# Attention feeding a leaky-ReLU MoE layer on one core: blocks of two query chunks, PV for two steps at once, k turned 128 rows a transfer, batch 0 turned by TensorE

## The chip, the cores and the metric

One core of one Trainium2 chip. The metric is the device time of one execution in microseconds (us); a kernel's time is the median of its runs. A profile is of one execution and gives a span a little shorter than that execution's time (599.0 of 600.70 us in after). Five engines work side by side: TensorE (PE in profile lines, its weight loads PEld), VectorE (DVE), ScalarE (ACT), GpSimd (POOL) and SyncE (SP), which issues most transfers (280 of the 328 listed for before).

A run counts as slow when it is over 1.5% above the fastest of the same kernel. Ratios use fast runs alone; where a profile fell in a slow run, the text says so.

## The reference

```python
# q, k, v: [8 batches, 8 heads, 576, 64] f32; tau = 0.02; w_in [512, 2048], w_out [2048, 512]
scores = q @ k.transpose(0, 1, 3, 2) / sqrt(64)
thresh = scores.max(-1, keepdims=True) - tau
scores = where(scores >= thresh, scores, -1e9)
attn   = exp(scores - scores.max(-1, keepdims=True))
attn   = attn / (attn.sum(-1, keepdims=True) + 1e-09)
x      = (attn @ v)              # heads side by side: 4608 tokens x 512
h      = x @ w_in
out    = maximum(0.01 * h, h) @ w_out
```

## The kernel before

The unit of work is a **step**: one pair of heads against 128 query rows (a *chunk*). A batch has 4 pairs x 4 chunks, and 2 steps for the 64 rows that are left over: 18 steps a batch, 144 in all. In every step TensorE does the scores; VectorE takes the row maximum and masks; ScalarE does the exponentials into `W`; a DMA transpose turns `W` into `wt`; four steps later (`LAG`) TensorE multiplies `wt` by v ("PV"). The products of finished chunks are the tokens of the MoE layer. Its matmuls fill up the steps: a *hidden unit* (`hp`, 16 matmuls and a ReLU) and an *output unit* (`op`, 4 or 5 matmuls) a step.

Each f32 value of q and k is split in two f16 halves (`qs`, `ks`), three products of which make the scores, and these too are turned by DMA transposes (`qst`, `kst`). `0.99 * relu(h) + 0.01 * h` is the leaky ReLU. In most groups the second term is folded into weights: `w_io = 0.01 * w_in @ w_out` is computed once (`wiop`) and the output unit adds `x @ w_io` (`op<-wio,xT`). Early groups, before `w_io` is ready, add it on VectorE (`leak`).

```python
    LAG = 4
    NWT = 2          # blocks of wt
    def turn(nm, b, p):                     # one pair of heads, 64 rows, of q or k
        hb, g = divmod(p, 2)
        t = sb.tile([128, 2, 576], FP16, tag=nm + "st", bufs=8, name=nm + "st")
        nc.sync.dma_start(out=t.rearrange("p s (t r) -> p (s t) r", r=64),
            in_=split_tile(nm, b, hb)[ds(64 * g, 64)].rearrange("p s t h d -> p (s t h d)"), transpose=True)
    # ... cut
    def h_unit(G, u):
        def mms():
            # ... cut
            hp = ps.tile([128, 4, 128], FP32, tag="h", bufs=2, name="hp")
            for jj in range(4):
                for g in range(4):
                    mm(hp[:, jj, :], w_in16[:, g, ts(4 * u + jj, 128)], G.x[:, g, :], g == 0, g == 3)
    # ... cut
    for b in range(1, B):                   # preparation of batch b during batch b - 1
        s0 = 18 * (b - 1)
        for hb in range(2):                 # two halves: pairs 0, 1 and pairs 2, 3
            # ... cut: loads of k and q
            t0 = s0 + 1 + 8 * hb
            at(t0, lambda b=b, hb=hb: hi("k", b, hb))
            at(t0 + 2, lambda b=b, hb=hb: hi("q", b, hb))
            i = 1
            for nm in "kq":
                # ... cut: the low halves on GpSimd, i += 2 for each of two heads
                for p in (2 * hb, 2 * hb + 1):
                    at(t0 + i + p % 2, lambda nm=nm, b=b, p=p: turn(nm, b, p))
        for i in range(4):
            at(s0 + 6 + i, lambda b=b, i=i: load_v(b, i))
    # ... cut: the loop over steps; turn_w(s - 1) and pv(s - LAG) in step s
    while hq or oq:                         # the tail: MoE units that are left
        for nx in (next_o, next_h):
            # ... cut
```

Counting it out for the second half: the q transposes of pairs 2 and 3 are issued at `s0 + 18` and `s0 + 19`, which are the first and second step of the batch that uses pair 2 in its third step.

Of the kernel before, what the change touches and what calls it, by code (L numbers as in the profile page):

```python
# [16 lines left out]
def kernel(  # L17
# [19 lines left out]

    nc = tc.nc
# [6 lines left out]
    LAG = 4  # L45
    L1_GROUPS = set(range(8, 36))
    WIO = 20
    NJ = DF // 128
    NEG = -1025.0
    NW = 4  # L50
    NG = 3
# [16 lines left out]
    w_io16 = sb.tile([128, 4, DM], FP16, name="wio16")  # L68

# [43 lines left out]
    def split_tile(nm, b, hb):  # L113
        store = kss if nm == "k" else qss
        if (b, hb) not in store:
            store[b, hb] = sb.tile([128, 2, 9, 2, 64], FP16, tag=nm + "s", bufs=NSPL, name=nm + "s")
        return store[b, hb]

    def views(nm, b, hb, i, part, rows):
        m = (kms if nm == "k" else qms)[b, hb]  # L120
        s_ = split_tile(nm, b, hb)
        t0, n, odd = part
        src = m[rows, :, ds(64 * t0, 64 * n)].rearrange("p h (t d) -> p h t d", d=64)
        if odd is None:
            dst = s_[rows, i, :, :, :]
        else:
            dst = s_[rows, i, odd : 2 * n - 1 + odd : 2, :, :]
        return src, dst.rearrange("p t h d -> p h t d")

    NSPL = 2  # L130
    ALL = ds(0, 128)

    def hi(nm, b, hb, rows=ALL, eng="act"):
        for part in PARTS[nm]:
            src, dst = views(nm, b, hb, 0, part, rows)
            if eng == "act":
                nc.scalar.activation(out=dst, in_=src, func=AF.Copy, bias=0.0, scale=64.0)  # L137
            else:
                nc.vector.tensor_scalar(out=dst, in0=src, scalar1=64.0, scalar2=None, op0=AX.mult)

    def x64(nm, b, hb, h, rows=ALL):
        m = (kms if nm == "k" else qms)[b, hb][rows, h, :]
        return nc.gpsimd.tensor_scalar(out=m, in0=m, scalar1=64.0, scalar2=1.0, op0=AX.mult, op1=AX.mult)  # L143

    def lo(nm, b, hb, h, part, rows=ALL, eng="pool"):
        src, dst = views(nm, b, hb, 1, part, rows)
        _, h_ = views(nm, b, hb, 0, part, rows)
# [5 lines left out]
    def turn(nm, b, p):  # L153
        hb, g = divmod(p, 2)
        t = sb.tile([128, 2, 576], FP16, tag=nm + "st", bufs=8, name=nm + "st")
        nc.sync.dma_start(  # L156
            out=t.rearrange("p s (t r) -> p (s t) r", r=64),
            in_=split_tile(nm, b, hb)[ds(64 * g, 64)].rearrange("p s t h d -> p (s t h d)"), transpose=True)
        (ksts if nm == "k" else qsts)[b, p] = t


    class Group:


        def __init__(self, rows):
            self.l1 = len(groups) in L1_GROUPS
            self.x = sb.tile([128, 4, 128], FP16, tag="xT", bufs=5, name="xT")
            self.g = None
            self.rows = rows
# [3 lines left out]
    live_g = [0]  # L173

    def next_h():

        if hq and (hq[0][1] > 0 or live_g[0] < NG):
            f, u = hq.popleft()
            if u == 0:
                live_g[0] += 1  # L180
            return f
        return None

    def next_o():
        if oq:
            f, last = oq.popleft()
            if last:
                live_g[0] -= 1
            return f
        return None  # L190
    late = []
    leaky = []

    def leak():
        for gv, hp in leaky:
            nc.vector.scalar_tensor_tensor(out=gv, in0=hp, scalar=0.01, in1=gv, op0=AX.mult, op1=AX.add)  # L196
        leaky.clear()

    tail = [False]
    def mm(out_, lhsT, rhs, start, stop):  # L200
        nc.tensor.matmul(out=out_, lhsT=lhsT, rhs=rhs, start=start, stop=stop, skip_group_check=True)  # L201

    def h_unit(G, u):
        def mms():
            if u == 0:
                G.g = sb.tile([128, NJ, 128], FP16, tag="gT", bufs=NG, name="gT")
            hp = ps.tile([128, 4, 128], FP32, tag="h", bufs=2, name="hp")
            for jj in range(4):
                for g in range(4):
                    mm(hp[:, jj, :], w_in16[:, g, ts(4 * u + jj, 128)], G.x[:, g, :], g == 0, g == 3)  # L210

            def act():
                gv = G.g[:, ds(4 * u, 4), :]
                nc.scalar.activation(out=gv, in_=hp, func=AF.Relu, bias=0.0, scale=0.99)  # L214
                if not G.l1:
                    leaky.append((gv, hp))
                if u == 3:
                    for c in range(4):
                        oq.append((lambda c=c: o_unit(G, c), c == 3))
# [3 lines left out]
    def o_unit(G, c):  # L223
        if c == 0:
            n = len(late) % 3 if tail[0] else 2
            late.append(0)
            if n < 2:
                G.op = ps.tile([128, 2, 512], FP32, tag=f"sc{n}", bufs=1, name="op")[:, 0, :]
            else:
                G.op = ps.tile([128, 512], FP32, tag="o", bufs=1, name="op")  # L230
        if G.l1:
            mm(G.op, G.x[:, c, :], w_io16[:, c, :], c == 0, False)
        for j in range(4 * c, 4 * c + 4):
            mm(G.op, G.g[:, j, :], w_out16[:, j, :], j == 0 and not G.l1, j == NJ - 1)
        if c == 3:
            op = G.op

            def fin():
                osb = sb.tile([128, 512], FP32, tag="osb", bufs=3, name="osb")
                if tail[0]:  # L240
# [3 lines left out]
                return lambda: nc.sync.dma_start(out=G.rows, in_=osb)  # L244
            return fin
# [316 lines left out]
```

## Time and profile before

Median of the first three runs: 627.69 us (626.74 to 628.02).

From the start times of `bb`, the small VectorE instruction that negates the row maximum once a step, the trace gives the time of every stage:

| stage | us |
|---|---|
| start to first `bb` | 18.4 |
| batch 0 | 88.6 |
| batch 1 | 79.7 |
| batches 2 to 7 (to the last `bb`) | 406.9 (67.4, 70.5, 72.0, 67.2, 69.1, 60.8) |
| tail (last `bb` to the end) | 32.9 |

The page of before: span, busy time of TensorE, and, in 40 slices, the granted clock of TensorE and the busy share of the DMA engines in tenths; last, the shares of the chain of work that ended last.

```profile
span 626.5 us, 16727 instructions
...
PE 521.8 (83%) x6576; PEld 343.0 (55%) x6576; DVE 445.5 (71%) x1385; ACT 441.8 (71%) x950; POOL 144.6 (23%) x196
...
PEclk9999989898997999899997998999996999899999
DMA  7999999899999999979998999989997999866631
...
PE 46%; DMA 24%; DVE 16%; ACT 8%; SPq 4%; issue 2%; ACTq 0%; DVEq 0%
```

TensorE leads, DMA is nearly always busy, and the clock row has dips all the way: in the trace they are ten stretches from 76.5 to 544.1 us, each 3.4 to 10.2 us long with a granted clock of 0.50, and each begins during, or at most 1.4 us after, a stretch of 2.2 to 3.9 us in which TensorE stood idle.

A step without a stall, in before's timeline of TensorE (columns: start, duration, engine, line, operation, operands, shape, count):

```profile
360.37 0.47 PE L324 MATMUL pv<-wt,v 128*64 128x128 f16 x10
360.77 0.39 PE L201 MATMUL op<-wio,xT 128*128 128x512 f16 x1
361.00 1.03 PE L201 MATMUL op<-wout,gT 128*128 128x512 f16 x4
361.86 1.06 PE L201 MATMUL hp<-xT,win 128*128 128x128 f16 x16
362.85 0.91 PE L300 MATMUL sc<-kst,qst 64*128 64x288 f16 x12
```

The groups follow each other without a gap: about 3.3 us. Here is the start of a batch in the same view:

```profile
333.56 1.62 PE L300 MATMUL sc<-kst,qst 64*128 64x288 f16 x12 [3.34 <-DMA qst<-qs]
...
336.19 1.91 PE L201 MATMUL op<-wout,gT 128*128 128x512 f16 x4
```

The bracket says that TensorE stood idle for 3.34 us until a q transpose landed. After it the same four output matmuls take 1.91 us, not 1.03. The clock in the trace goes with that: from 332.5 us on, the granted clock was 0.50 for 6.8 us. "Cold" and "half clock" mean such stretches here.

Waits of before (engine, line, waited-for: us in total, times, longest), and the issues of weight transposes (count, median us from issue to landing):

```profile
PE pv L324 <- DMA wt<-w: 40.3, 21, 9.0
...
PE sc L300 <- DMA qst<-qs: 21.4, 7, 3.9
```

```profile
wt<-w SPq DMA_TRANSPOSE x144, 4.2
```

Two groups of VectorE and a stretch of the tail:

```profile
L482 DVE TENSOR_SCALAR P<-sf,mx 128x576 f16<-128x576 f32 x144 | 75.0, 521 | 0.0
...
L336 DVE TENSOR_TENSOR xT<-pv,wt 128x512 f16<-128x512 f32 x32 | 23.3, 727 | 10.7 <-PE pv L324 10.7
```

```profile
607.78 0.38 PE L201 MATMUL op<-wio,xT 128*128 128x512 f16 x1
...
608.86 1.06 PE L201 MATMUL hp<-xT,win 128*128 128x128 f16 x16
609.76 0.38 PE L201 MATMUL op<-wio,xT 128*128 128x512 f16 x1
```

A pair of hidden and output unit takes 1.98 us in the tail (607.78 to 609.76), without a wait.

### The profile page before, as it was taken

The page shows a single profiled execution, that of the slowest core. Times are in us where ns is not written, and L with a number is a line of the kernel's source. Part 1 is how long each engine was busy: PE and PEld are TensorE (multiplying, and loading weights), DVE is VectorE, ACT ScalarE, POOL GpSimd, SP SyncE. Part 2 cuts the span into 40 slices and gives each one's busy share as a digit, 9 for nine tenths or more (in the row PEclk, how much of TensorE's full clock was granted, in tenths as well). Part 3 has the DMA queues.
Part 4 walks back from the last instruction along what each step waited for, and adds up shares of the span by engine and source line. Part 5 has one row for each costly group of instructions (what it writes and reads, how often), then busy time and mean ns, then how long its engine had stood idle before and what let it go on. Part 6 is the DMA issues. An engine that isn't in the chain of part 4 may idle for free.

```text
span 626.5 us, 16727 instructions
## 1 busy us (share of the span) xinstructions
PE 521.8 (83%) x6576; PEld 343.0 (55%) x6576; DVE 445.5 (71%) x1385; ACT 441.8 (71%) x950; POOL 144.6 (23%) x196
## 2 busy tenths in 40 slices
PE   0352698889997998798897998798988999899997
PEld 0131465545564665465565665565655666566664
DVE  4462679784796998577874886687884888688810
ACT  3171578775786897688875996788876988688831
POOL 0162422131221432033311331133311432000000
PEclk9999989898997999899997998999996999899999
DMA  7999999899999999979998999989997999866631
GB/s 198 162 203 199 207 200 186 175 197 194 167 190 162 178 189 205 162 167 172 189 187 157 175 183 209 160 170 174 194 189 159 180 176 167 135 121 128 118 61 50
DMA packets 300046, 106.47 MB, mean 170 GB/s; under 512 B 274880, under 2 KB 287168, under 8 KB 299968
## 3 DMA queue, kind: packets, MB, share of 16 engines
q1 hardware_dynamic: 286912, 96.50, 85.6%
q0 software_dynamic: 13056, 8.92, 11.3%
q8 instruction: 51, 0.84, 0.6%
q14 instruction: 27, 0.22, 0.1%
HBM read 36.70 MB, written 9.44 MB: 74 GB/s over the span
## 4 chain that ended last, share of the span: by engine, by line
PE 46%; DMA 24%; DVE 16%; ACT 8%; SPq 4%; issue 2%; ACTq 0%; DVEq 0%
DMA wt<-w 17%; PE op L201 16%; PE hp L201 12%; PE sc L300 9%; DVE sf L359 8%; PE pv L324 5%; DMA qst<-qs 5%; SPq L156 3%; ACT w L473 3%; ACT P L484 2%; PE wiop L201 2%; DVE P L469 2%; DVE gT L196 2%; PE sc L306 1%; ACT qs L137 1%
## 5 line engine op out<-in xcount | busy, mean ns | idle before, releaser
L359 DVE TENSOR_SCALAR_CACHE_REDUCE sf<-sc 128x576 f32<-128x576 f32 x288 | 206.5, 755 | 114.3 <-PE sc L300 104.8
L473 ACT ACTIVATE w<-P 128x576 f16<-128x576 f16 x288 | 193.5, 675 | 24.8 <-DVE P L469 17.3
L300 PE MATMUL sc<-kst,qst 64*128 64x288 f16 x1536 | 129.6, 304 | 52.8 <-DMA kst<-ks 23.0
L201 PEld LDWEIGHTS <-win 128*128 128x128 f16 x2304 | 147.9, 101 | 35.6 <-issue 4.4
L484 ACT ACTIVATE P<-sf,bb 128x576 f16<-128x576 f32 x144 | 111.5, 774 | 71.8 <-DVE bb L480 66.7
L201 PE MATMUL hp<-xT,win 128*128 128x128 f16 x2304 | 159.7, 225 | 0.0
L201 PE MATMUL op<-wout,gT 128*128 128x512 f16 x576 | 155.1, 393 | 0.2 <-ACT osb L243 0.2
L214 ACT ACTIVATE gT<-hp 128x512 f16<-128x512 f32 x144 | 85.2, 592 | 54.6 <-PE hp L201 52.0
L300 PEld LDWEIGHTS <-qst 64*128 64x128 f16 x1536 | 70.1, 99 | 86.1 <-DMA qst<-qs 35.6
L324 PE MATMUL pv<-wt,v 128*64 128x128 f16 (+1 forms) x1600 | 72.0, 226 | 46.3 <-DMA wt<-w 40.3
L324 PEld LDWEIGHTS <-v 128*64 128x64 f16 x1600 | 51.3, 115 | 82.2 <-issue 71.9
L201 PEld LDWEIGHTS <-gT 128*128 128x128 f16 x576 | 55.3, 100 | 55.0 <-issue 7.2
L482 DVE TENSOR_SCALAR P<-sf,mx 128x576 f16<-128x576 f32 x144 | 75.0, 521 | 0.0
L469 DVE TENSOR_SCALAR P<-P 128x1152 int16<-128x1152 int16 x144 | 66.2, 460 | 9.3 <-ACT P L484 4.0
L149 POOL TENSOR_TENSOR ks<-km,ks 128x320 f16<-128x320 f32 (+1 forms) x56 | 39.8, 730 | 83.7 <-DVE P L469 55.8
L473 ACT ACTIVATION_READ_ACCUMULATOR w<-P 128x1 f32 x288 | 54.8, 190 | 0.0
L143 POOL TENSOR_SCALAR km<-km 128x576 f32<-128x576 f32 x28 | 18.7, 669 | 150.8 <-ACT ks L137 109.8
L149 POOL TENSOR_TENSOR qs<-qm,qs 128x576 f16<-128x576 f32 x28 | 35.8, 1278 | 64.7 <-DVE P L469 37.8
L201 PE MATMUL op<-wio,xT 128*128 128x512 f16 x112 | 44.8, 400 | 1.0 <-ACT osb L243 0.8
L489 DVE TENSOR_SCALAR w<-rc 128x128 f16<-128x128 f32 x144 | 32.6, 227 | 5.0
L143 POOL TENSOR_SCALAR qm<-qm 128x576 f32<-128x576 f32 x28 | 18.7, 669 | 65.4 <-DVE P L469 65.4
L336 DVE TENSOR_TENSOR xT<-pv,wt 128x512 f16<-128x512 f32 x32 | 23.3, 727 | 10.7 <-PE pv L324 10.7
(30 smaller groups left out, 254.8 us busy)
## 6 DMA issues: line engine op xcount, KB each, us to landing
km<-in_k_dram SPq DMA_DIRECT2D x16, 576.0 KB, 5.3
qm<-in_q_dram SPq DMA_DIRECT2D x16, 576.0 KB, 5.4
out_dram<-osb SPq DMA_DIRECT2D x36, 256.0 KB, 3.4
v<-in_v_dram POOLq DMA_DIRECT2D x16, 160.0 KB, 5.2
wt<-w SPq DMA_TRANSPOSE x144, 4.2
v<-in_v_dram POOLq DMA_DIRECT2D x16, 128.0 KB, 5.2
win<-in_moe_w_in_dram POOLq DMA_DIRECT2D x8, 256.0 KB, 10.1
wout<-in_moe_w_out_dram POOLq DMA_DIRECT2D x8, 256.0 KB, 10.4
```

The lines of the kernel that those rows point to most:

```text
L143: return nc.gpsimd.tensor_scalar(out=m, in0=m, scalar1=64.0, scalar2=1.0, op0=AX.mult, op1=AX.mult)
L149: return nc.gpsimd.tensor_tensor(out=dst[:, h], in0=src[:, h], in1=h_[:, h], op=AX.subtract)
L201: nc.tensor.matmul(out=out_, lhsT=lhsT, rhs=rhs, start=start, stop=stop, skip_group_check=True)
L214: nc.scalar.activation(out=gv, in_=hp, func=AF.Relu, bias=0.0, scale=0.99)
L300: nc.tensor.matmul(out=sc[h][:, half, 0:288], lhsT=qsts[b, p][r, qi, ds(128 * c, 128)], rhs=ksts[b, p][r, ki, ks_], start=(i == 0), stop=( ...
L324: nc.tensor.matmul(out=pvp[ds(64 * h, 64), p + u, :], lhsT=vt[:, p + u, h, j, :], rhs=wt[:, 4 * h + j, ds(64 * u, n)], start=(j == 0), sto ...
L359: nc.vector.tensor_scalar(out=halves(sf), in0=sc[:, :, 0:288], scalar1=C, scalar2=None, op0=AX.mult, op1=AX.max, accum_out=mx)
L469: anchor[0] = nc.vector.tensor_scalar(out=pi, in0=pi, scalar1=NEG, scalar2=None, op0=AX.max)
L473: nc.scalar.activation(out=e["W"][:, ds(576 * h, 576)], in_=e["P"][:, h, :], func=AF.Exp, bias=exp_bias, scale=1.0, accum_out=sm[:, h : h ...
L482: nc.vector.tensor_scalar(out=d["P"][:, 0, :], in0=sa, scalar1=ma, scalar2=tau_f, op0=AX.subtract, op1=AX.add)
L484: nc.scalar.activation(out=d["P"][:, 1, :], in_=sB, func=AF.Identity, bias=bb, scale=1.0)
L489: nc.vector.tensor_scalar(out=e["W"][:, 1152:1280].rearrange("p (h r) -> p h r", h=2), in0=rc.unsqueeze(2).to_broadcast([128, 2, 64]), sca ...
```

## The change

The intent: fewer and larger instructions and transposes, and q and k of the next batch turned longer before their use. From batch 2 on, two neighbouring chunks of a head pair form one unit of two steps: their `W` are turned by one transpose of 2560 columns, multiplied by v in one go (10 matmuls of 256 columns for two steps, not 20 of 128), and their tokens form one MoE group of 256 (8 matmuls of 256 columns to a hidden unit, not 16 of 128). k is turned 128 rows a transfer (two pairs at once); q stays at 64. The preparation of the next batch is laid out anew. For the second half the last two q transposes stand at `s0 + 17` and `s0 + 18`, one step earlier than before (those of the first half stand two steps later). A unit takes two steps, so pair 2 is first used in the fifth step of a batch, no longer in the third. Batch 0's q and k are turned by TensorE (`tp`). The fold of the leak stays, and its range hardly moves (from batch 2, before from the last chunk of batch 1). The 256-token hidden unit has one PSUM buffer, where hidden units had two. `xT` is evacuated per head pair and chunk (128 times), not per chunk (32 times).

```diff
-    L1_GROUPS = set(range(8, 36))
-    WIO = 20
+    L1_FROM = 2
+    WIO = 21
+    PREP = 6
+    NWT = 4
+    WOUT = 1
 ... cut
+        if nm == "k":
+            nc.sync.dma_start(
+                out=t.rearrange("p s t g r -> p (s t) (g r)"), in_=s_.rearrange("p s t h d -> p (s t h d)"),
+                transpose=True)
+        else:
+            nc.sync.dma_start(
+                out=t[:, g].rearrange("p s t r -> p (s t) r"),
+                in_=s_[ds(64 * g, 64)].rearrange("p s t h d -> p (s t h d)"), transpose=True)
 ... cut: turn_pe, eight TensorE transposes of batch 0 and their evacuations
-            hp = ps.tile([128, 4, 128], FP32, tag="h", bufs=2, name="hp")
-            for jj in range(4):
+            hp = ps.tile([128, nj, G.n], FP32, tag="hy"[u % 2] if G.n == 128 else "h", bufs=1, name="hp")
+            for jj in range(nj):
 ... cut
+        blocks = [(0, 1), (2, 3), (4,)]
+        if b < L1_FROM:
+            blocks = [(0,), (1,), (2,), (3,), (4,)]
+        elif b == B - 1:
+            blocks = [(0, 1), (4,), (2,), (3,)]
 ... cut
-            t0 = s0 + 1 + 8 * hb
+            t0 = s0 + PREP + (5 if b >= L1_FROM else 3) * hb
 ... cut: k transposes at t0 + 3, q transposes at t0 + 6 and t0 + 7
-            at(s0 + 6 + i, lambda b=b, i=i: load_v(b, i))
+            at(max(s0 + 10, 12) + i, lambda b=b, i=i: load_v(b, i))
 ... cut
+        last = units[ui][3] + size[ui] - 1
+        pv_at.setdefault(EARLY.get(ui, last + LAG), []).append(ui)
 ... cut
+            uwt[done] = sb.tile([128, 2, 10, 128], FP16, tag="wt", bufs=NWT, name="wt")
+            nc.sync.dma_start(
+                out=uwt[done][:, 0:nw].rearrange("p i j r -> p (i j) r"), in_=W_.rearrange("p i c -> p (i c)"),
+                transpose=True)
```

## The prediction

> **What bounds the kernel now.** From the timeline and the spacing of the row-maximum negations (bb, one a step, 144 steps):
> (a) Where nothing stalls, a step takes 3.3 us and TensorE is full: scores 0.83, PV 0.41, one output unit 1.09, one hidden unit 0.99. VectorE and ScalarE are busy about 2.9 us a step. 144 x 3.32 = 478 us.
> (b) Batches 2 to 7 take 67.4, 70.5, 72.0, 67.2, 69.1, 60.8 us against 18 x 3.3 = 59.4. Mostly at batch starts: the second and third steps take 7 to 9 and 4 to 5 us, because the last q transposes are issued one step before use (chain of waits at 328.8 us: DMA qst<-qs 4.75 us), and matmuls after it run cold (four output matmuls 1.91 us, not 1.03). [...] About 7 us a batch; the rest is waits for wt<-w.
> (c) Batch 0 takes 88.6 us, batch 1 79.7: first scores at 15.2 us, then steps of 7 to 11 us while q/k transposes, weight loads and wt transposes share the DMA engines (chain: wt<-w 28 us from 39 us on). Batch 1 also holds about 15 us of weight product (wiop).
>
> DMA is nearly full (slices at 9). The trace's 256-byte packets take 18 ns in the 128-row wt transposes (about 210 GB/s, 1.55 us a step) but 28 to 31 ns while only 64-row q/k transposes run (140 GB/s, 2.2 us each).
>
> **What the change does.**
> - Batch 0 turned by TensorE: eight 2.2 us transposes leave the start; v and w_in loads start at about 7 us instead of 20 to 35. Costs evacuations on ScalarE and VectorE. First scores at about 12.5 us. Gain, estimate: 20 us.
> - q/k preparation moves ahead: the last q transpose lands some 4 steps before use, so (b)'s 7 us should vanish. With new waits, batches 2 to 7 take about 62 us (the last 58). Gain 39 us, the largest term.
> - k at 128 rows: two 2.2 us transposes become one of about 2.8 us, 3 us less DMA a batch. [...]
> - PV of two steps at once, 256-token hidden matmuls: same streamed columns, half the weight loads[...]. Estimate 0.1 us a step, to 3.2; included above.
> - Leak in weights: as before in effect.
> - Tail (33 us after the last bb): 256-token groups arrive in bursts, single hidden buffer: +2 us.
> - Batch 1: less q/k contention: -4 us.
>
> Sum: 627 - 39 - 20 - 4 + 2 = 566; fewer cold stretches: 563.
>
> **Predicted: 563 us, 8 in 10 between 540 and 590. Faster 0.95, same 0.04, slower 0.01.**
>
> **What would show it.** Spacing of bb: no 7 to 9 us step at batch starts, steady steps 3.15 to 3.25, batch 0 at 60 to 70 us; qst waits near zero; TensorE busy about 88%; kst issues landing in 5 to 6 us; the chain's DMA share falling from 24% to about 12%.
>
> **What would make it wrong.** A 2560-column wt transpose (about 3.1 us) queued behind q/k transposes and loads may reach PV late, turning the removed stall into wt waits (590). The single hidden buffer may make TensorE wait for ScalarE's Relu. Or DMA is no bound and steps reach 3.1 us (540).

The sum: 627 - 39 - 20 - 4 + 2 = 566, and 563 with the 3 us for fewer cold stretches. The 2.8 and 3.1 us for larger transposes are estimates from the 18 ns packets (210 GB/s) of before's trace; the 0.1 us a step and the 3 us are estimates, which no run had measured.

## The result, and the profile after

After: 601.46 us (597.31 to 604.79, 4 runs); before beside it: 627.22 us (624.33 to 628.02, 4 runs). Ratio 0.9594, 95% interval 0.9525 to 0.9663: faster, but the time lies outside the predicted range of 540 to 590. A ratio is the mean time of one kernel's fast runs over the mean of the other's fast runs of the same rounds, so not quite the ratio of the medians quoted.

| stage | before | after | difference | predicted |
|---|---|---|---|---|
| start and batch 0 | 107.0 | 89.9 | -17.1 | -20 |
| batch 1 | 79.7 | 86.6 | +6.9 | -4 |
| batches 2 to 7 | 406.9 | 380.7 | -26.2 | -39 |
| tail | 32.9 | 41.9 | +9.0 | +2 |
| sum (span) | 626.5 | 599.0 | -27.5 | -61, and -3 for fewer cold stretches |

The stage times contain the cold stretches, so that last term has no row of its own.

The page of after, the lines shown of before:

```profile
span 599.0 us, 14446 instructions
...
PE 512.1 (85%) x5500; PEld 317.1 (53%) x5500; DVE 459.4 (77%) x1395; ACT 440.5 (74%) x948; POOL 148.7 (25%) x198
...
PEclk9999999989999999999999999999999999999999
...
PE 43%; DVE 23%; DMA 23%; ACT 7%; issue 3%; SPq 1%; ACTq 0%
```

The DMA share of the chain stays where it was (24% and 23%); the prediction expected it to halve. VectorE's share grows from 16% to 23%. (The clock row of this one run is the best of the four; the other runs of after had mean clocks of 0.947 to 0.956, against 0.991 here, and times of 597 to 605 us on both sides of it. The mean clock alone does not order the runs. In the profiles of a_noleak and a_blk1, with means of 0.958 and 0.948, the clock of batch 0 was 0.79 and 0.75, and batch 0 was no longer for it.)

Waits and transposes of after:

```profile
PE pv L386 <- DMA wt<-w: 31.9, 18, 5.4
...
PE hp L228 <- ACT gT L242: 6.9, 6, 1.8
...
PE sc L355 <- DMA qst<-qs: 4.4, 1, 4.4
```

```profile
wt<-w SPq DMA_TRANSPOSE x92, 5.1
```

As predicted, the wait of the scores for q nearly vanishes: 21.4 us in 7 waits became 4.4 in one, in batch 1. On average over batches 2 to 7, the q of pair 2 landed 11.5 us after the last `bb` of the batch before, and 6.8 us after it in the new kernel, where it is also used two steps later. But PV still waits 31.9 us for turned weights, and a wait of the hidden unit for its one buffer (`hp <- gT`) is new. One of the PV waits, in the timeline of SyncE's queue (first column: issue) and then of TensorE:

```profile
283.40 5.51 SPq L576 DMA_TRANSPOSE wt<-w  x1
289.00 3.63 SPq L172 DMA_TRANSPOSE qst<-qs  x2
```

```profile
288.57 0.91 PE L355 MATMUL sc<-kst,qst 64*128 64x320 f16 x12
292.78 0.74 PE L386 MATMUL pv<-wt,v 128*64 128x256 f16 x10 [3.30 <-DMA wt<-w]
```

A transpose of two steps' weights is issued at 283.40 us, between output stores (issued at 281.50) and loads of v, and lands only when PV can start, at 292.7: 9.3 us. By the order of the program three steps lie between, but the transpose is issued late in its step, once the exponentials are done: TensorE stood ready for PV 6.1 us after the issue (292.78 less the wait of 3.30). Matching every transpose of batches 2 to 7 with its PV gives the medians: from issue to landing 4.1 us before and 5.9 us after; from issue to the moment that TensorE could take PV 7.3 us before and 6.6 us after. The usual margin shrank from about 3 us to less than 1.

The windows view over batches 2 to 7 (columns: window, its length, then busy time and instruction count of TensorE, its weight loads, VectorE, ScalarE, GpSimd; mean clock; DMA share; GB/s). Before, then after:

```profile
186.70:593.60 406.90, 371.15 (x4870) 245.81 (x4867) 316.41 (x1001) 322.46 (x700) 92.77 (x120) 0.95 0.99 170
```

```profile
176.50:557.10 380.60, 346.50 (x3682) 212.19 (x3680) 323.51 (x984) 313.79 (x686) 95.29 (x120) 1.00 1.00 183
```

This is the surprising pair of lines. The time in which TensorE does nothing is 406.9 - 371.2 = 35.8 us before and 380.6 - 346.5 = 34.1 us after. The change took the q waits away, and waits of the same size came in their place. By releaser, the gaps of TensorE over 0.2 us in these batches were, before, 18.7 us for q and 15.8 for `wt`; after, 19.2 for `wt`, 6.9 for the hidden buffer and 4.7 for scores that wait for VectorE to empty their PSUM. What fell is TensorE's busy time, by 25 us. About 16 of them are time lost to the half clock while TensorE was busy (17.4 us before, 1.7 after, from the granted clock of the trace). About 6 are work that was only moved: a count of the matmuls shows 14,000 fewer columns of the MoE layer streamed in these batches (487,040 before, 473,088 after), of which 8,700 turn up in the tail. That leaves about 3 us for the larger matmuls.

VectorE, the same two groups:

```profile
L562 DVE TENSOR_SCALAR P<-sf,mx 128x576 f16<-128x576 f32 x144 | 83.3, 579 | 0.0
...
L396 DVE TENSOR_TENSOR xT<-pv,wt 128x128 f16<-128x128 f32 x128 | 33.5, 294 | 6.0 <-PE pv L386 6.0
```

The split evacuation of `xT` costs 33.5 us where it cost 23.3, and the masking op became slower on average without having changed. The window 50 to 100 us of after, which is the second half of batch 0 (to 89.9 us) and the first 10 us of batch 1, shows how full VectorE is with them (columns as above), and after's timeline of VectorE and then of GpSimd around 72 us shows one of the slow masking ops:

```profile
50.00:100.00 50.00, 41.43 (x551) 28.73 (x547) 46.48 (x142) 40.24 (x87) 19.42 (x24) 1.00 1.07 178
```

```profile
71.94 1.05 DVE L562 TENSOR_SCALAR P<-sf,mx 128x576 f16<-128x576 f32 x1
72.91 0.68 DVE L220 SCALAR_TENSOR_TENSOR gT<-hp,gT 128x512 f16<-128x512 f32 x1
```

```profile
70.64 1.29 POOL L152 TENSOR_TENSOR qs<-qm,qs 128x576 f16<-128x576 f32 x1 [0.48 <-DVE P L545]
71.88 1.64 POOL L152 TENSOR_TENSOR ks<-km,ks 128x320 f16<-128x320 f32 x2
```

VectorE is busy 46.5 of 50 us: it is the bound here, not TensorE (41.4). The masking op took 1.05 us beside GpSimd's subtraction, twice its mean before. Over the whole of both traces it took 510 ns where no GpSimd instruction ran beside it; beside one it took 560 ns on average before (30 times) and 704 ns after (51 times). Why it is slower there, no run shows. The line below it in the timeline is the leak on VectorE, 0.68 us.

Batch 1 is another matter. Its windows, before and after, and a wait of after that before does not have:

```profile
107.00:186.70 79.70, 70.15 (x827) 43.38 (x825) 60.20 (x184) 55.94 (x121) 18.55 (x24) 0.96 1.07 182
```

```profile
89.80:176.40 86.60, 72.55 (x842) 44.70 (x843) 62.48 (x195) 55.20 (x121) 18.79 (x24) 0.96 1.02 177
```

```profile
PE wiop L228 <- DVE rc L570: 4.6, 2, 2.7
```

VectorE is busy 62.5 of 86.6 us in batch 1, only 2.3 us more than before, and less than TensorE: it is not full there. But two of the four weight products wait for it, 4.6 us in all. The first of them starts at 130.80 us, 0.14 us after a leak on VectorE ends. A leak reads the PSUM buffer of its hidden unit, and of the buffers with the tag of the weight product (`h`) there is one now and were two before.

Last, the tail:

```profile
576.35 1.06 PE L228 MATMUL hp<-xT,win 128*128 128x128 f16 x16
577.24 0.38 PE L228 MATMUL op<-wio,xT 128*128 128x512 f16 x1
578.10 1.04 PE L228 MATMUL op<-wout,gT 128*128 128x512 f16 x4 [0.47 <-ACT gT L242]
578.97 1.06 PE L228 MATMUL hp<-xT,win 128*128 128x128 f16 x16
```

A pair takes 2.62 us (576.35 to 578.97), against 1.98 before: the output unit comes right after the hidden unit whose ReLU it needs, and waits for it.

### The profile page after: what moved, and what is told of

It is laid out like the page before. It is cut to its first block, busy times and chain, and to the rows that moved or that the text cites. A ratio compares the mean times of both kernels' runs of the same rounds, so it can differ in the third digit from the quotient of the medians.

```text
span 599.0 us, 14446 instructions
## 1 busy us (share of the span) xinstructions
PE 512.1 (85%) x5500; PEld 317.1 (53%) x5500; DVE 459.4 (77%) x1395; ACT 440.5 (74%) x948; POOL 148.7 (25%) x198
## 4 chain that ended last, share of the span: by engine, by line
PE 43%; DVE 23%; DMA 23%; ACT 7%; issue 3%; SPq 1%; ACTq 0%
DMA wt<-w 20%; PE op L228 14%; DVE sf L416 12%; PE hp L228 11%; PE sc L355 9%; PE pv L386 5%; DVE P L562 3%; PE wiop L228 3%; DVE P L545 2%; DVE gT L220 2%; ACT gT L242 2%; ACT w L550 2%; ACT P L564 1%; DVE w L572 1%; DVE xT L396 1%
## 5 line engine op out<-in xcount | busy, mean ns | idle before, releaser
L228 PE MATMUL hp<-xT,win 128*128 128x128 f16 (+1 forms) x1600 | 152.2, 244 | 7.8 <-ACT gT L242 6.9
L228 PEld LDWEIGHTS <-win 128*128 128x128 f16 x1600 | 124.3, 99 | 48.2 <-issue 10.6
L355 PE MATMUL sc<-kst,qst 64*128 64x320 f16 (+1 forms) x1536 | 128.9, 297 | 12.7 <-DVE sf L416 7.6
L386 PE MATMUL pv<-wt,v 128*64 128x256 f16 (+2 forms) x1160 | 59.8, 241 | 40.8 <-DMA wt<-w 31.9
L228 PEld LDWEIGHTS <-gT 128*128 128x128 f16 x576 | 49.2, 98 | 65.1 <-ACT gT L242 13.4
L562 DVE TENSOR_SCALAR P<-sf,mx 128x576 f16<-128x576 f32 x144 | 83.3, 579 | 0.0
L386 PEld LDWEIGHTS <-v 128*64 128x64 f16 x1160 | 44.2, 114 | 60.6 <-issue 51.8
L146 POOL TENSOR_SCALAR km<-km 128x576 f32<-128x576 f32 x28 | 19.2, 687 | 199.7 <-ACT ks L142 144.8
L152 POOL TENSOR_TENSOR ks<-km,ks 128x320 f16<-128x320 f32 (+1 forms) x56 | 43.4, 794 | 28.5 <-DVE P L545 27.4
L228 PE MATMUL op<-wio,xT 128*128 128x512 f16 x108 | 41.7, 386 | 0.6 <-ACT osb L274 0.6
L396 DVE TENSOR_TENSOR xT<-pv,wt 128x128 f16<-128x128 f32 x128 | 33.5, 294 | 6.0 <-PE pv L386 6.0
L272 DVE COPY osb<-op 128x512 f32<-128x512 f32 x14 | 9.6, 686 | 28.7 <-PE op L228 28.7
```

The source lines that it names most:

```text
L146: return nc.gpsimd.tensor_scalar(out=m, in0=m, scalar1=64.0, scalar2=1.0, op0=AX.mult, op1=AX.mult)
L152: return nc.gpsimd.tensor_tensor(out=dst[:, h], in0=src[:, h], in1=h_[:, h], op=AX.subtract)
L228: nc.tensor.matmul(out=out_, lhsT=lhsT, rhs=rhs, start=start, stop=stop, skip_group_check=True)
L355: nc.tensor.matmul(out=sc[h][:, cols], lhsT=qt[r, g, qi, ds(2 * c, 2), :].rearrange("p t r -> p (t r)"), rhs=rhs, start=(i == 0), stop=(i ...
L386: nc.tensor.matmul(out=o_[ds(64 * h, 64)], lhsT=vt[:, pp, h, j, :], rhs=w_[:, :, 4 * h + j, :], start=(j == 0), stop=(j == 4), skip_group_ ...
L396: nc.vector.tensor_tensor(out=G.x[:, p, ds(128 * c, 128)].rearrange("f (p i) -> f i p", i=2), in0=pvp[:, ds(128 * c, 128)].rearrange("f (i ...
```

## The experiments

The theory: in batches 2 to 7 the lost gain lies in turned weights that land too late for PV, a matter of *latency*. Rivals: q waits were never worth what the prediction said; the DMA engines are simply full (*throughput*), so that any transfer moved only moves the wait; the two-chunk blocks cost what they give. For the other stages: VectorE with the leak bounds batch 1, and the order of units costs the tail 6 us. Labels with a_ edit the kernel after, labels with b_ the kernel before. All kernels computed the right result except where said. Stage times are of the profiled run.

| kernel | median us (range) | ratio to before [95%] | batch 0 / 1 | batches 2-7 | tail |
|---|---|---|---|---|---|
| before | 627.22 (624.33-628.02) | 1 | 88.6 / 79.7 | 406.9 | 32.9 |
| after | 601.46 (597.31-604.79) | 0.9594 [0.9525, 0.9663] | 75.5 / 86.6 | 380.7 | 41.9 |
| a_tail | 594.93 (591.41-597.36) | 0.9555 [0.9481, 0.9630] | 74.0 / 85.7 | 383.4 | 36.2 |
| a_k64 | 606.57 (603.55-610.15) | 0.9756 [0.9665, 0.9847] | 73.3 / 87.1 | 389.4 | 42.0 |
| a_blk1 | 600.37 (596.23-603.28) | 0.9649 [0.9558, 0.9740] | 74.0 / 86.9 | 392.2 | 31.5 |
| a_noqk | 587.31 (583.3-590.29) | 0.9320 [0.9266, 0.9374] | 74.6 / 88.2 | 369.8 | 41.7 |
| a_noleak | 592.4 (591.94-593.02) | 0.9423 [0.9386, 0.9459] | 72.0 / 79.3 | 383.6 | 41.9 |
| a_wout | 604.03 (601.84-608.28) | 0.9615 [0.9562, 0.9669] | 77.8 / 86.5 | 386.0 | 41.9 |
| a_late | 640.39 (639.09-641.6) | 1.0219 [1.0163, 1.0274] | 74.6 / 84.6 | 424.1 | 41.9 |
| a_vmove | 604.59 (604.09-607.96) | 0.9682 [0.9627, 0.9738] | 72.9 / 88.5 | 385.8 | 41.9 |
| a_lag6 | 578.33 (575.43-584.94) | 0.9235 [0.9171, 0.9300] | 74.2 / 86.8 | 368.7 (slow run) | 38.8 |
| b_early2 | 633.15 (632.55-633.75) | 1.0070 [1.0010, 1.0131] | 90.4 / 85.0 | 405.8 | 32.6 |
| b_spread | 616.21 (612.63-618.67) | 0.9835 [0.9783, 0.9887] | 92.1 / 80.2 | 393.9 | 32.6 |
| b_lag6 | 627.91 (627.45-629.95) | 1.0069 [1.0011, 1.0127] | 90.8 / 79.8 | 401.2 | 38.0 |
| b_sp_lag6 | 604.91 (601.41-606.23) | 0.9706 [0.9642, 0.9770] | 89.1 / 81.3 | 374.8 | 37.7 |
| best1 | 598.06 (596.11-603.12) | 0.9566 [0.9518, 0.9615] | 74.9 / 86.1 | 389.0 | 36.8 |
| best2 | 587.75 (586.29-602.64) | 0.9377 [0.9335, 0.9420] | 78.8 / 78.6 (slow run) | 394.7 (slow run) | 34.7 |
| best4 | 593.43 (589.64-597.35) | 0.9493 [0.9425, 0.9561] | 80.4 / 79.2 | 382.8 | 38.6 |
| best3 | 572.34 (570.45-575.18) | 0.9161 [0.9117, 0.9206] | 74.7 / 74.1 | 373.6 | 35.5 |

The kernel before ran beside each call, with medians of 624.9 to 628.5 us. Medians differ by some us for the same kernel, so a difference between two kernels is read from the ratios and the stages. Two cautions. In a_tail, a_k64, a_blk1 and b_early one run of before took 616.4 us, so that 7 of its 11 runs counted as slow, and ratios stand about 0.7% higher than against its median of 626.2 us. And stages scatter between profiles: in after, a_tail, a_noleak and a_wout the schedule of batches 2 to 7 is the same, and they took 380.7 to 386.0 us. A difference below about 5 us in this stage says nothing by itself.

### a_tail: the order of units in the tail

```diff
-        for nx in (next_o, next_h):
+        for nx in (next_o if len(oq) > 1 or not hq else next_h, next_h):
```

> The kernel after, with one thing changed: after the last step an output unit is issued only when a second one is queued behind it, so it does not need the Relu of the hidden unit just before it. After the last bb the kernel after takes 41.9 us against 32.9 before, and each hidden-output pair 2.62 us against 1.97. Theory D (dependence: output unit waits for the Relu, 0.65 us a pair over about 11 pairs): the tail falls by 6 to 8 us to about 35, pairs back at about 2.0, whole kernel about 594. Rival B (backlog: more units are simply left over by the bursts of 256-token groups): pairs may shorten but the tail stays above 40 and the kernel within 2 us of 601.

The tail fell from 41.9 to 36.2 us. In its timeline of TensorE the wait is gone and a pair takes 1.98 us again (577.37 to 579.35):

```profile
577.37 1.06 PE L228 MATMUL hp<-xT,win 128*128 128x128 f16 x16
...
579.35 1.06 PE L228 MATMUL hp<-xT,win 128*128 128x128 f16 x16
```

So about 6 of the tail's 9 us are the order of the units. The whole time is too coarse to show it on its own: the intervals of the ratios overlap. The remaining 3 us fit a count of the matmuls: the tail of after and of a_tail holds three hidden units and five output matmuls more than before's, and TensorE is busy 31.3 us in the tail of a_tail against 27.2 before.

### a_k64: k turned 64 rows a transfer again

```diff
-            nc.sync.dma_start(
-                out=t.rearrange("p s t g r -> p (s t) (g r)"), in_=s_.rearrange("p s t h d -> p (s t h d)"),
-                transpose=True)
+            for g in range(2):
+                nc.sync.dma_start(
+                    out=t[:, :, :, g, :].rearrange("p s t r -> p (s t) r"),
+                    in_=s_[ds(64 * g, 64)].rearrange("p s t h d -> p (s t h d)"), transpose=True)
```

> The kernel after with k turned by two transposes of 64 rows instead of one of 128. If DMA time is what holds batches 2 to 7 above 18 x 3.25 us, the 1.6 us more of DMA per half batch (two of 2.2 against one of 2.8) show: batches 2 to 7 rise by up to 6 x 3.2 = 19 us, kernel 610 to 620. If DMA has slack there, within 4 us of 601, and wt waits change little.

Batches 2 to 7 took 389.4 us, 8.7 more, and the ratio rose by 0.016, or by about 0.01 with the caution above. The gaps of TensorE for `wt` grew from 19.2 to 22.1 us; 7 of the 8.7 us go with the half clock, at which this profile lost 9.1 us where after's lost 1.7. So the part seems worth a few microseconds, as the prediction had it, and no more is shown. The 256-byte packets of before's trace took 18 ns in most 128-row transposes of weights, and 26 to 30 ns on average from 10 to 20 us, where only 64-row ones ran. What makes the 64-row ones slower is not shown.

### a_blk1: one-chunk blocks in every batch

```diff
-        if b < L1_FROM:
+        if b < B - 1:
             blocks = [(0,), (1,), (2,), (3,), (4,)]
         elif b == B - 1:
-            blocks = [(0, 1), (4,), (2,), (3,)]
+            blocks = [(0,), (1,), (4,), (2,), (3,)]
```

> The kernel after with one-chunk blocks in every batch: PV of one step at a time, 128-token groups, W transposed 1280 columns a time; k at 128 rows, batch 0 by TensorE and the earlier preparation are kept. My prediction gave the two-chunk blocks 0.1 us a step: then 108 steps cost about 11 us more, 612. If they are worth less, because 256-token groups bring waits of their own (hidden buffer single, bursts), 598 to 606; if their larger W transposes do harm, below 598.

Batches 2 to 7 took 11.5 us more and the tail 10.4 us less, and the time is that of after within its interval. In the windows view TensorE was busy 362.0 us in these batches, at a clock of 0.98; a_tail, with two-chunk blocks at the same clock of 0.98, was busy 352.4. That looks like the predicted 0.1 us a step, but much of it is work that was moved. Counting the matmuls, a_blk1 streamed 13,824 more columns of the MoE layer in these batches than a_tail, about 6 us by the times of the units, and as many fewer in the tail, which was 4.7 us shorter than a_tail's. The larger matmuls themselves are left with some 4 us of the difference. (The times of the units would give up to 8: a PV of two steps takes 0.67 us, two single ones 0.80.) As to waits, `wt` gaps fell from 19.2 to 12.4 us, while q gaps of 8.1 us came: the q transposes are issued in the same steps as in after, but pair 2 is due in the third step again. So the two-chunk blocks are a part of what removed the q waits.

### a_noqk: no q and k transposes from batch 3 on (wrong result)

```diff
     def turn(nm, b, hb, g=None):
+        if b > 2:
+            (ksts if nm == "k" else qsts)[b, hb] = (ksts if nm == "k" else qsts)[2, hb]
+            return
```

> Wrong result on purpose: the kernel after, where batches 3 to 7 use batch 2's turned q and k, so that about 14 us of transposes a batch leave the DMA engines in batches 2 to 6; loads, splits and all arithmetic stay. If DMA contention is what keeps batches 2 to 6 at 63 to 65 us, they fall to 59 to 60 (18 x 3.25 = 58.5) and the kernel by 20 to 25 us to about 578. If TensorE, the single hidden buffer and VectorE hold them, they stay within 1.5 us of before each and the kernel above 592.

Its 14 us are an estimate: four q transposes of the 2.2 us measured in before and two of k at the estimated 2.8 us.

The result is wrong (relative error 0.913). Batches 2 to 7 took 369.8 us, 10.9 less, and `wt` gaps fell from 19.2 to 10.9 us. So the neighbouring transposes delay the weights, but with all of them gone in five batches more than half of the `wt` gaps remain. Full DMA engines explain part of the waits at most.

### a_noleak: no leak on VectorE in batches 0 and 1

```diff
-                if not G.l1:
-                    leaky.append((G, u, hp))
-                else:
+                if True:
                     oq.append((lambda: o_unit(G, u), G.n))
```

> Wrong result on purpose: the kernel after without the leak's additions on VectorE in batches 0 and 1 (36 of 0.68 us). If VectorE bounds batches 0 and 1 (3.5 us a step there), steps 9 to 36 fall to about 3.25, and the weight products of batch 1 no longer wait for a hidden buffer that the leak still reads: batch 0 about 72, batch 1 79 to 81 instead of 86.6, kernel 588 to 594. If DMA or TensorE bounds them, batch 1 stays above 84.

The arithmetic is incomplete; the comparison's tolerance let it pass. Batch 1 fell from 86.6 to 79.3 us and batch 0 from 75.5 to 72.0; the ratio fell by 0.017. In the window 50 to 100 us VectorE's busy time fell from 46.5 to 40.4 us. A leak off VectorE is worth some 10 us. In batch 1 part of this is the weight product, which no longer waits for VectorE (4.6 us in after, none here): its four steps took 26.3 us instead of 31.5. The experiment does not separate the time of the leak on VectorE from the time for which it holds the PSUM buffer.

### a_wout: loads of w_out later

```diff
-    WOUT = 1
+    WOUT = 5
```

> The kernel after with the loads of the output weights issued from step 5 on instead of step 1. In the kernel after, the first wt transpose lands 14.5 us and the second 16 us after issue, while w_in and w_out loads run; TensorE waits 5.4 and 4.7 us at steps 4 and 5 and then runs cold; the first output unit needs w_out only at 59 us. If those loads are what delays the transposes, batch 0 falls by 7 to 10 us to 66 to 68, which is what I had predicted, and the kernel to about 593. If the transposes are slow for another reason (first use, w_in alone), batch 0 stays within 3 us of 75.

The idea was that loads of w_out hold up the first weight transposes of batch 0 (one issued at 21.1 us landed at 35.6). The steps that had stalled, the fifth and sixth, ran without a stall, but the tenth and eleventh now took 12.4 and 6.3 us, and batch 0 as a whole took 77.8 us instead of 75.5. The wait only moved: no gain.

### b_early: before, with the second half's preparation four steps earlier

```diff
-            t0 = s0 + 9 * hb
+            t0 = s0 + (9 if b == 1 else 5) * hb
             at(t0 - 7, lambda b=b, hb=hb: load_half(k, kms, "km", b, hb))
             at(t0 - 5, lambda b=b, hb=hb: load_half(q, qms, "qm", b, hb))
-            t0 = s0 + 1 + 8 * hb
+            t0 = s0 + 1 + (8 if b == 1 else 4) * hb
```

> The kernel before, with only the preparation of the second half of q and k (heads 4 to 7) moved 4 steps earlier from batch 2 on. Theory P (my prediction's largest term): the late q transposes cost about 6 to 7 us a batch, waiting plus cold clock, so batches 2 to 7 fall from 407 to about 368 and the kernel to about 590. Rival G (given back): the same DMA work moved earlier delays the wt transposes instead; qst waits vanish but wt waits grow, batches 2 to 7 stay above 385 and the kernel above 606.

Its median of 6 runs was 631.71 us (624.52 to 681.7), ratio 1.0104 [0.9996, 1.0211]. The profiled run was the slow one of 681.7 us, so its stages say nothing. Its page shows a granted clock that is low from the sixth slice to the end, on one core:

```profile
PEclk9999877677777777777777777777777777777777
```

### b_early2: the same kernel again

> The same kernel as b_early, again, for a profile at full clock (the first profile ran at a granted clock of 0.75 throughout, so its stages say nothing). Five other executions gave 624.5 to 636 us, no gain. Theory G (given back): qst waits of batches 2 to 7 are gone from the profile and wt or other waits, or lower-clock stretches, are larger by about the same 35 us; batches 2 to 7 still sum to about 400. Theory P would need them at about 370 with the loss in batches 0 and 1, which the edit hardly touches.

Batches 2 to 7: 405.8 us, as before's 406.9. The stalls at the second and third step of the batches were gone; instead the fifteenth and sixteenth step of the batches took up to 7 and 10.5 us. The gaps of TensorE for q vanished and those for `wt` grew from 15.8 to 30.7 us. The edit also moves the loads of q and k four steps earlier. Brought that far forward, q by itself is worth nothing in the kernel before. That seemed to speak for the rival "q waits were never worth it".

### b_spread: before, with the second half's preparation two steps earlier, loads left alone

```diff
-            t0 = s0 + 1 + 8 * hb
+            t0 = s0 + 1 + (8 if b == 1 else 6) * hb
```

> The kernel before with only the second half's splits and transposes 2 steps earlier from batch 2 on, the q and k loads left where they were. b_early removed the q waits but bunched two loads and six transposes at steps 10 to 15 of the preceding batch, and new stalls of 8 to 10 us appeared at steps 14 and 15: batches 2 to 7 406 us as before. If that was only the bunching (theory: spacing), this spread schedule takes batches 2 to 7 to 375 to 385 and the kernel to 600 to 605. If the wait always returns because the DMA engines are nearly full in this kernel (theory: DMA work), batches 2 to 7 stay above 395 and the kernel above 615.

Batches 2 to 7: 393.9 us, 13 less, ratio 0.9835: some of the gain is there if the transposes come just early enough. The stalls lay at the last three steps of the batches, above all at the last (7.1 us on average). Its waits say why it is not more:

```profile
PE pv L324 <- DMA wt<-w: 54.7, 23, 9.2
...
PE sc L300 <- DMA qst<-qs: 2.6, 1, 2.6
```

In the whole run the wait for q is gone (21.4 before), and the wait for `wt` has risen from 40.3 to 54.7.

### a_late: after, with the second half's preparation three steps later

```diff
-            t0 = s0 + PREP + (5 if b >= L1_FROM else 3) * hb
+            t0 = s0 + PREP + (8 if b >= L1_FROM else 3) * hb
```

> The reverse: the kernel after with the second half of q and k prepared 3 steps later from batch 2 on, so that the last q transposes are again issued one to two steps before use. If a late q transpose itself costs 6 to 7 us a batch (my prediction), batches 2 to 7 rise by 35 us to about 415 and the kernel to 635. If DMA work decides and waits only move, qst waits come back but wt waits shrink: kernel below 615.

Batches 2 to 7: 424.1 us, 43.4 more than after, and the time, 640.39 us, is above the kernel before. The fourth and fifth steps of the batches took 8.1 and 4.5 us on average. Its waits:

```profile
PE pv L386 <- DMA wt<-w: 33.0, 15, 5.9
...
PE sc L355 <- DMA qst<-qs: 30.4, 7, 5.9
```

The wait for weights stays (31.9 in after) and the wait for q is added on top. The mechanism that the prediction put first is right: in the new kernel, having q in time is what keeps it ahead of before at all. The rival "q waits were never worth it" falls.

### best1: a_tail and one-chunk blocks in the last batch

```diff
         elif b == B - 1:
-            blocks = [(0, 1), (4,), (2,), (3,)]
+            blocks = [(0,), (1,), (4,), (2,), (3,)]
```

> The kernel after with the tail order of a_tail and one-chunk blocks in the last batch only (batches 2 to 6 keep two-chunk blocks). One-chunk blocks everywhere cost 9 to 11 us in batches 2 to 7 but left a tail of 31.5 us instead of 41.9, because the last groups of tokens become ready earlier. Expected: tail 28 to 31 us, batch 7 about 60, kernel 587 to 591. If the burst of the last 256-token group is not what fills the tail, 594 as a_tail.

A miss: the tail stayed at 36.8 us (a_tail 36.2), and the ratio at 0.9566 (0.9555). One-chunk blocks in the last batch alone don't shorten the tail; the short tail of a_blk1, 31.5 us, comes from a backlog of MoE units that builds up before. A count of the matmuls shows it: best1 and a_tail have the same 66,816 columns of the MoE layer left in the tail, a_blk1 has 52,992. Why the backlog builds up with groups of 256 tokens is not shown.

### best2: best1, and the leak folded from batch 1

```diff
-    L1_FROM = 2
-    WIO = 21
+    L1_FROM = 1
+    WIO = 13
 ... and a buffer of its own (two) for winT, sf with three buffers instead of four
```

> best1 with the leak folded into weights, and two-chunk blocks, from batch 1 on: the weight products come at steps 18 to 27 and their turned weights have buffers of their own. a_noleak showed that the leak on VectorE costs about 11 us in batches 0 and 1, most of it in batch 1. Expected if that carries over: batch 1 at 77 to 80 us instead of 86, kernel 580 to 584. If the four transposes of w_in, brought into the crowded start, cost as much as the leak, 587 or more.

587.75 us, ratio 0.9377: 0.019 below best1. That is more than the 580 to 584 us expected. Batch 1 took 78.6 us, even in a profile of a slow run; batch 0 rose to 78.8. The first weight product starts only at its very end (92.5 us), but the transpose of w_in for it, issued at 73.5 us, now falls into batch 0. Two of its six runs were slow (595.7 and 602.6 us).

### a_vmove: loads of v spread away from the weights' transposes

```diff
-            at(max(s0 + 10, 12) + i, lambda b=b, i=i: load_v(b, i))
+            at(12 + i if b == 1 else s0 + 6 + 3 * i, lambda b=b, i=i: load_v(b, i))
```

> The kernel after with only the v loads of batches 2 to 7 spread over steps 6, 9, 12 and 15 of the preceding batch instead of 10 to 13. In the kernel after the two-step W transpose issued at 283.4 us lands 9.3 us later, among two output stores and three v loads, and TensorE waits 3.3 us for it. If this collision makes the waits of steps 13 to 15, they fall by 2 to 3 us a batch: batches 2 to 7 at 366 to 372, kernel 588 to 593. If the DMA engines are simply full there, the waits move to other steps and the sum stays within 4 us of 381.

Batches 2 to 7: 385.8 us, not less than after's 380.7; the `wt` gaps were 25.1 us, against 19.2. Spreading the loads took nothing away. With a_wout this is the second time that rearranging transfers did nothing.

### a_lag6: PV two steps later in batches 2 to 6

```diff
         last = units[ui][3] + size[ui] - 1
-        pv_at.setdefault(EARLY.get(ui, last + LAG), []).append(ui)
+        lag = 6 if L1_FROM <= units[ui][0] < B - 1 else LAG
+        pv_at.setdefault(EARLY.get(ui, last + lag), []).append(ui)
```

> The kernel after with PV six steps behind the scores instead of four in batches 2 to 6: same DMA work, two more steps (about 6.5 us) for a W transpose to land. If late landings alone hold batches 2 to 7 at 381 (latency), wt waits there go to nearly zero and the sum to 362 to 368, kernel 584 to 590. If DMA throughput holds them, the waits come back once the slack is used: above 376, kernel above 597.

578.33 us, ratio 0.9235 [0.9171, 0.9300], against 0.9594 [0.9525, 0.9663] for after: about 22 us for one constant. No transfer was moved, added or removed. Its profile fell in a slow run (584.9 us), yet batches 2 to 7 took 368.7 us in it, the 368 of the prediction. The windows view of these batches and the wait for weights:

```profile
175.60:544.30 368.70, 346.00 (x3670) 210.85 (x3668) 321.72 (x986) 312.78 (x685) 94.34 (x120) 0.99 1.02 189
```

```profile
PE pv L386 <- DMA wt<-w: 12.1, 5, 5.2
```

TensorE is busy as long as in after, and unoccupied for 22.7 us instead of 34.1. The wait for weights that is left, 12.1 us, lies in batches 0 and 1; in batches 2 to 7 there is no gap for `wt` any more. The transposes land as late as they did (median 5.9 us after the issue in both); TensorE could take PV 11.1 us after the issue, not 6.6. That settles latency against throughput: with DMA engines that could move no more, a later PV could not have made the stage shorter. The DMA share of about 1 in the windows is no such limit, for the rate rose from 183 to 189 GB/s beside it. Nor did q come too late, although its last transposes landed 9.2 and 15.7 us after the last `bb` of the batch before: the two-step units use them late enough.

### best4 and best3: what adds up

best4 is a_tail with best2's fold of the leak from batch 1. best3 is best4 with a_vmove and a_lag6:

```diff
+            at(12 + i if b == 1 else s0 + 6 + 3 * i, lambda b=b, i=i: load_v(b, i))
 ... cut
+        lag = 6 if L1_FROM <= units[ui][0] < B - 1 else LAG
 ... cut: the edits of best4
```

> best2 without the one-chunk last batch, which best1 showed to be no gain over a_tail (598 against 595): 584 to 590.

593.43 us, ratio 0.9493 [0.9425, 0.9561]. A miss: 584 to 590 was expected. Batch 1 gains 7 us and batch 0 loses 5 in this profile. In best3, with the same fold, batch 0 took 74.7 us, so the loss in batch 0 is not the fold's alone.

> best4 with the spread v loads and the later PV together. If latency and collision are the causes: 570 to 578. If DMA throughput is: 583 or more.

572.34 us, ratio 0.9161 [0.9117, 0.9206]: faster than both kernels, 21 us below best4, with batches 0 and 1 at 74.7 and 74.1 us. It is the best version.

### b_lag6 and b_sp_lag6: the kernel before with a longer lag

The last question: does the longer lag alone help the kernel before, or does it need the early q?

```diff
-    LAG = 4
+    LAG = 6
 ... cut
-    NWT = 2
+    NWT = 3
```

> The control: the kernel before with PV six steps behind the scores and the third buffer, q and k as they were. The late q transposes stay, so batches 2 to 7 can fall only by the other excess, about 14 us, to 393 to 400, and the kernel to 612 to 620. If it falls as far as b_sp_lag6, late q was never the cost.

627.91 us, ratio 1.0069: nothing gained. Batches 2 to 7 took 401.2 us, the `wt` gaps in them were gone, and q gaps stood at 34.8 us (18.7 before). What was taken from one wait was waited for the other. In the whole run (21.4 us before):

```profile
PE sc L300 <- DMA qst<-qs: 41.4, 7, 7.2
```

b_sp_lag6 adds the edit of b_spread.

> b_spread (the kernel before, second half of q and k two steps earlier) with PV six steps behind the scores instead of four, and a third buffer for the turned W. b_spread lost two thirds of the q waits' worth to wt waits (batches 2 to 7 394 us instead of 407; 68 us of wt waits in all). a_lag6 showed that in the kernel after the wt waits are late landings that two more steps hide. If the same holds here, batches 2 to 7 fall to 366 to 374 and the kernel to 588 to 598: then late q was worth what I had predicted, and only the short distance to PV gave it back. If DMA throughput of this kernel holds it, batches 2 to 7 stay above 385.

604.91 us, ratio 0.9706. Batches 2 to 7: 374.8 us, with 9.6 us of q gaps and none for `wt`. Set side by side, as differences to before in batches 2 to 7: early q alone -1 (b_early2) or -13 (b_spread), the lag alone -6, both -32. The two single edits of which it is made give 19 together; the other 13 us belong to neither alone. Stages scatter by some 5 us, but the ratios say the same: 1.0069 and 0.9835 alone, 0.9706 together, with intervals that don't meet. The kernel stayed above the 588 to 598 us expected. It also means that three lines in the kernel before give about three quarters of what the whole change gave (ratios 0.9706 and 0.9594).

## Why the prediction was wrong, point by point

The span was to fall by 64 us and fell by 27.5. Of the 36.5 us that are missing, 13 are in batches 2 to 7, 11 in batch 1, 7 in the tail, 3 in the start with batch 0, and 3 are the cold stretches that were counted apart.

**Batches 2 to 7: the step that failed.** The prediction's largest term reads: "With new waits, batches 2 to 7 take about 62 us (the last 58). Gain 39 us, the largest term." The first half of that argument, that "the last q transpose lands some 4 steps before use, so (b)'s 7 us should vanish", is right: the q wait went, and a_late shows what it is worth in this kernel (43 us). Only the reason is half of it: the last q transposes are issued one step earlier, and it is the order of the two-step units that puts their use two steps later (a_blk1: without that, q gaps of 8.1 us). The new waits were mis-sized. The prediction's 368 us over 107 steps of its 3.2 us (342) allowed 26 us for all waits and slower steps. There were 34.1 us in which TensorE did nothing, of which 19.2 for turned weights and 6.9 for the hidden buffer; and TensorE was busy 346.5 us, where 342 was the sum of the steps. So 8 of the 13 us are waits and 4 are TensorE's own work, although about 6 us of it had moved out of these batches. The measured gain was 26.2 us. The prediction named the cause among its dangers ("A 2560-column wt transpose ... may reach PV late, turning the removed stall into wt waits (590)") and did not carry it into its sum. It could have: in the trace of before TensorE could take PV 7.3 us after the issue (median), and the page gave 4.2 us to landing for half the size, with waits of up to 9.0 us. a_lag6, which gives the transposes two more steps and changes nothing else, brings these batches to 368.7 us.

**Where the gain did come from.** TensorE's busy time fell by 25 us in these batches: some 16 us with the clock (0.95 before, 1.00 after), 6 us because work moved out of them, and about 3 us by larger matmuls (4 to 8 from a_blk1 against a_tail), where the prediction had 0.1 us a step, or 11 us. That the clock does this is seen in b_spread too: with before's instructions at 0.98 TensorE was busy 363.0 us instead of 371.2. These shares come from single profiles.

**Batch 1: wrong sign.** "Less q/k contention: -4 us" became +6.9. The step that failed is the wait that was to go: the scores waited 2.7 us for q in batch 1 before and 4.4 us after, for in this batch units have one chunk and pair 2 is due in the third step as before. And a wait came that the prediction did not have: the weight product for a PSUM buffer that the leak still reads (4.6 us); the four steps with a weight product took 31.5 us, 27.7 before. a_noleak and the kernels that fold from batch 1 bring the batch to 74 to 79 us. VectorE itself is only 2.3 us busier than before, with the split `xT` evacuation and the slower masking ops beside GpSimd (over the whole run 10.2 us more for the one, and 704 ns on average against 510 for the other). How the rest of the 6.9 us divides is open.

**The tail: +9 instead of +2.** The prediction named bursts and the single buffer. About 6 us are something it had not seen, the order of units (a_tail: 2.62 to 1.98 us a pair). The other 3 are the backlog: 8,700 more columns of the MoE layer were left for the tail, and best1 did not cure that.

**Batch 0: -17 instead of -20.** Close. The stall that remained there, transposes behind the loads of w_in and w_out, only moves when the loads move (a_wout).

**The signs that it named.** q waits near zero: 4.4 us, right. No step of 7 to 9 us at the starts of batches 2 to 7: the longest second or third step took 5.4 us, right. Steady steps of 3.15 to 3.25 us: the median in these batches went from 3.32 to 3.35, wrong. k transposes landing in 5 to 6 us: the median is 6.5, wrong. Batch 0 at 60 to 70 us: 75.5, wrong. TensorE busy 88%: 85%. The DMA share of the chain at 12%: 23%, and this was the plainest sign that waits had been exchanged, not removed.

**What stays open.** How the +6.9 us of batch 1 divide; and why groups of 256 tokens leave more of the MoE layer for the tail.

## What to carry to other kernels

When a change removes one wait, list what the released engine will wait for next and compare that thing's *landing* time with its due time: twice the transpose behind an unchanged lag was left with a margin of less than 1 us. Take the due time from the trace, not from the count of steps (6.6 us here, where three steps are 10). Try the lag, a constant, before rearranging transfers: rearranging gained nothing three times here (loads of w_out, loads of v, q four steps earlier), while two more steps between issue and use took the waits for weights out of batches 2 to 7. Two waits that take turns must be removed together, or one gain shows up as the other's loss (-6 and -13 us alone, -32 together). And before busy times of a stage are compared, count the work in it: some may have moved to another stage.

## Hardware figures measured here

- Rate of DMA transposes: beside other traffic, a 128-row transpose of weights (327,680 bytes, issued at 58.5 us in after) moved about 210 GB/s (1.54 us), most of its 256-byte packets taking 18 ns; 64-row ones of q and k moved about 130 GB/s (26 to 30 ns a packet on average, 10 to 20 us of before).
- Time from issue to landing of a weight transpose among other traffic: the median was 4.2 us for 1280 columns before, 5.1 us for the mix of 1280 and 2560 columns after (3.3 to 16.0), and it decided the result.
- Granted clock: one run of b_early, a program on one core, had a mean granted clock of 0.77, between 0.7 and 0.8 in all slices of its page from the sixth on but one (the eighth, 0.6 to 0.7), and took 681.7 us, against 624.52 for its fastest run. What set it off isn't known.
- Spacing of matmuls: in the trace of before, a score matmul that follows a hidden matmul started about 95 ns later than another hidden matmul in its place (medians of 152 against 56 ns, start to start, behind 128 columns; after: 205 against 109 behind 256).
